# Expert blocks behind a dense layer: DMA transposes for the first three blocks, a later place for the last gate, and a list table read from another queue

## The chip, the cores and the metric

One core of a Trainium2 chip runs the kernel. The metric is the device time of one execution in microseconds; lower is better. The core's engines work in parallel and each takes its own instructions in order: TensorE (PE, matmuls; PEld are its weight loads), VectorE (DVE), ScalarE (ACT), GpSimd (POOL) and SyncE (SP, which here only issues transfers). Sixteen DMA engines carry out the transfers that SyncE and GpSimd issue.

## The reference: what is computed

```python
x = attention(q, k, v)                 # 4 x 8 heads, 576 positions, decaying mask, no softmax -> [2304, 512]
x = softplus(x @ w_in) @ w_out         # dense layer, 512 -> 2048 -> 512
logits = x @ w_gate                    # 8 experts
noisy = logits + log1p(exp(x @ w_noise)) * noise
top2 = argpartition(-noisy, 2, axis=1)[:, :2]
w = exp(top2_logits - max);  w /= w.sum() + 1e-9
for e in range(8):                     # each token goes to two experts
    h = maximum(x[mask_e] @ w1[e], 0)  # 512 -> 1024
    out[mask_e] += w[mask_e] * (h @ w2[e])
```

## The kernel before

The 2304 tokens are worked in six tiles of 384 (`NTILE`, `TT`). Numbers that need float32 are held as a high and a low half in float16, and a product is three matmuls (high with high, low with high, high with low).

**The dense layer.** `g1` and `g2` run tile by tile in a list of steps. When a tile's rows are done, `x2_done` (three times, j = 0 to 2) writes them as float16 rows, has SyncE transpose them by DMA into `x2t` and store them in the DRAM tensor X2. `logits(t)` multiplies the transposed rows with the gate's weights (36 matmuls of 16 columns, L432), takes the top two, builds `M` (which experts a token takes) and the running counts `mc`, and the exp and reciprocal for the weights. `ranks(t)` turns counts into each token's place in its expert's list (six matmuls, L471 and L472), and GpSimd scatters six columns of entries (token, weight) into the DRAM `table` (L504).

**The lists.** `schedule(first, n)` turns the counts into a list of blocks: for each block its table column, its expert's place and whether its weights have to be loaded. It is made twice: list a holds the first `NBA` = 5 blocks and is made from the counts of five of the six tiles, list b holds the other 39 and is made when the last tile's counts are known. In both cases the whole table is read into `tab` (L603, 380 KB, on SyncE).

**The expert blocks.** A block is 128 entries of one expert, some 36 to 44 in all. `prep(i)` copies the block's entries out of `tab` on GpSimd (L646), gathers the rows from X2 (L649), and has SyncE transpose them by DMA into `xt` (L655, 128 x 1024 float16). `e1(i)` is the first layer: two halves of 12 matmuls (L668), each evicted by ScalarE as the high part (L673) and by VectorE as the low part (L674) of `hr`, interleaved; then VectorE transposes `hr` into `ht` with 16 instructions (L680). `e2(i)` is the second layer, 24 matmuls (L689) on `ht`, and `combine(i)` scales the result on ScalarE (L700) and adds it to the output with an indirect DMA on GpSimd (L701). `weights(i, half)` is a 2 MB load on SyncE under a condition (L637): it moves bytes only where the block's expert differs from that of the block before. `e2` lags `e1` by three blocks (`LAG`).

**What sets the order.** The instructions are traced in program order; a planner then fills each engine's queue by its own model of times: of the instructions that it takes to be ready it takes the one traced first. So later work may be put ahead of earlier work that is not ready by that model. `tc.issue_after(x)` puts the instructions of a block behind `x` on the same engine, and `behind("sync")` puts them behind the last instruction noted as `LAST["sync"]`, here a DMA transpose. Around the change the program traces: the last rows of the dense layer, `prep(0)` to `prep(3)` (`PA` = 4) with the first weight load between, `logits(5)`, block 0's `e1`, weight loads, `ranks(5)`, block 1's `e1`, one more `prep`, list b with block 2's `e1` in its middle, and then the loop over blocks.

Of the kernel before, what the change touches and what calls it, by code (L numbers as in the profile page):

```python
# [10 lines left out]
F32 = mybir.dt.float32  # L11
F16 = mybir.dt.float16
# [4 lines left out]
AF = mybir.ActivationFunctionType  # L17
ALU = mybir.AluOpType

B, H, S, D = 4, 8, 576, 64  # L20
NT, DM, FF = 2304, 512, 2048
NE, F2 = 8, 1024
# [9 lines left out]
NBLK = 2 * NT // P + NE  # L32
NB = NT // P
NBA = 5
NTAIL = 3
NCOL = NE * NB + NBLK + 2

# [43 lines left out]
def body(ctx, tc, ins, out):  # L81
# [324 lines left out]
    MC = {0: rt.tile([P, 4, NE], F16, name="mc", bufs=2)}  # L406
    nc.vector.memset(MC[0], 0.0)

    XT2, RT, STORE, SCAT = {}, {}, {}, {}

    def x2_done(t, j):
        end = t == NTILE - 1
        rows = E["ep"].tile([P, 2, DM], F16, name="rows", bufs=3) if end else ring("rows", 1, 0, [2, DM], F16, 3)
        p2 = PG.pop((t, j))
        k = S_X2 / (S_G * S_WO)
        nc.scalar.activation(rows[:, 0], p2, AF.Copy, scale=k)
        nc.vector.scalar_tensor_tensor(out=rows[:, 1], in0=p2, scalar=k, in1=rows[:, 0], op0=ALU.mult, op1=ALU.subtract)
        r = rows.rearrange("p a d -> p (a d)")
        xt = E["ep"].tile([P, 8, P], F16, name="x2t", bufs=3) if end else ring("x2t", 1, 6144, [8, P], F16, 3)
        nc.sync.dma_start_transpose(out=xt, in_=r)  # L420
        t0 = t * TT + j * P
        STORE[t, j] = nc.sync.dma_start(out=X2[t0:t0 + P, :], in_=r)
        XT2[t, j] = xt

    def logits(t):
        lg = ps.tile([P, 3, 16], F32, tag="sm", name="lg", bufs=1)
        for j in range(3):
            xt = XT2.pop((t, j))
            n = 0
            for k in range(KC):  # L430
                for a, b in ((0, 0), (0, 1), (1, 0)):
                    nc.tensor.matmul(lg[:, j, :], lhsT=xt[:, a * 4 + k, :], rhs=wg[:, b, k, :], start=n == 0, stop=n == 11)  # L432
                    n += 1
        s = 1.0 / (S_X2 * S_WG)
        ns = rt.tile([P, 3, NE], F32, name="ns", bufs=2)
        nc.scalar.activation(ns, lg[:, :, 8:16], AF.Exp, scale=s)
        nc.scalar.activation(ns, ns, AF.Ln, bias=1.0)
        nc.vector.tensor_tensor(out=ns, in0=ns, in1=noise[:, 3 * t:3 * t + 3, :], op=ALU.mult)
        nl = rt.tile([P, 3, NE], F32, name="nl", bufs=2)
        nc.vector.scalar_tensor_tensor(out=nl, in0=lg[:, :, 0:8], scalar=s, in1=ns, op0=ALU.mult, op1=ALU.add)  # L440
        mx = rt.tile([P, 3, NE], F32, name="mx", bufs=2)
        ix = rt.tile([P, 3, NE], U32, name="ix", bufs=2)
        for j in range(3):
            nc.vector.max(out=mx[:, j], in_=nl[:, j])
            nc.vector.max_index(out=ix[:, j], in_max=mx[:, j], in_values=nl[:, j])
        ef = rt.tile([P, 3, 2], F32, name="ef", bufs=2)
        nc.vector.tensor_copy(ef, ix[:, :, 0:2])
        oh = rt.tile([P, 3, 2, NE], F16, name="oh", bufs=2)
        nc.vector.tensor_tensor(out=oh, in0=iota[:, None, None, :NE].to_broadcast([P, 3, 2, NE]),
                                in1=ef[:, :, :, None].to_broadcast([P, 3, 2, NE]), op=ALU.is_equal)  # L450
        M = rt.tile([P, 3, NE], F16, name="M", bufs=2)
        nc.vector.tensor_tensor(out=M, in0=oh[:, :, 0], in1=oh[:, :, 1], op=ALU.add)
        mc = MC[t]
        for j in range(3):
            nc.vector.tensor_tensor(out=mc[:, j + 1], in0=mc[:, j], in1=M[:, j], op=ALU.add)
        MC[t + 1] = rt.tile([P, 4, NE], F16, name="mc", bufs=2)
        nc.vector.tensor_copy(MC[t + 1][:, 0], mc[:, 3])

        ed = rt.tile([P, 3, 4], F32, name="ed", bufs=2)
        nc.vector.tensor_tensor(out=ed[:, :, 0], in0=mx[:, :, 1], in1=mx[:, :, 0], op=ALU.subtract)  # L460
        nc.scalar.activation(ed[:, :, 1], ed[:, :, 0], AF.Exp)
        nc.vector.tensor_scalar(ed[:, :, 2], ed[:, :, 1], 1.0, 1e-9, op0=ALU.add, op1=ALU.add)
        nc.vector.reciprocal(ed[:, :, 3], ed[:, :, 2])
        RT[t] = (ef, oh, M, ed)

    def ranks(t):
        ef, oh, M, ed = RT.pop(t)
        mc = MC.pop(t)
        pr = ps.tile([P, 3, NE], F32, tag="sm", name="pr", bufs=1)
        for j in range(3):  # L470
            nc.tensor.matmul(pr[:, j], lhsT=before, rhs=M[:, j], start=True, stop=False)  # L471
            nc.tensor.matmul(pr[:, j], lhsT=ones, rhs=mc[:, j], start=False, stop=True)  # L472
        qe = rt.tile([P, 3, NE], F32, name="qe", bufs=2)
        nc.vector.tensor_tensor(out=qe, in0=pr, in1=e4k[:, None, :].to_broadcast([P, 3, NE]), op=ALU.add)
        pq = rt.tile([P, 3, 2, NE], F32, name="pq", bufs=2)
# [43 lines left out]
    def schedule(first, n, between=lambda: None):  # L519
# [80 lines left out]
            LIST["more"] = ni[0:1, 0:1]  # L600
            nc.vector.tensor_scalar(ni[:, 0:1], red(nb[:, None, :]), float(n - NTAIL), None, op0=ALU.is_gt)
        tab = E["ep"].tile([P, NCOL * 4], I32, name="tab", bufs=1)
        nc.sync.dma_start(out=tab, in_=table.rearrange("(p c) f -> p (c f)", p=P))  # L603
        return bi, tab


# [48 lines left out]
        LAST["sync"] = nc.sync.dma_start_transpose(out=xt, in_=xr)  # L655
        TI[i], XE[i] = ti, xt

    def e1(i):
        ep, r, xt = E["ep2"], REG[i], XE.pop(i)
        hr = ep.tile([P, 2 * F2], F16, name="hr", bufs=3)  # L660
        pair = hr.rearrange("p (f a) -> p f a", a=2)
        M1[i] = []
        for n in range(2):
            ph = E["eps" if i < NBA else "eps2"].tile([P, 512], F32, name="ph", bufs=2)
            m = 0
            for k in range(KC):
                for a, b in ((0, 0), (1, 0), (0, 1)):
                    M1[i].append(nc.tensor.matmul(  # L668
                        ph, lhsT=xt[:, a * 4 + k, :], rhs=AR[0][:, ds(r * 8192 + (b * 4096 + k * 1024 + n * 512), 512)],
                        start=m == 0, stop=m == 11))  # L670
                    m += 1
            hi, lo = (pair[:, n * 512:(n + 1) * 512, a] for a in range(2))
            LAST["act"] = nc.scalar.activation(hi, ph, AF.Relu)  # L673
            nc.vector.scalar_tensor_tensor(out=lo, in0=ph, scalar=0.0, in1=hi, op0=ALU.max, op1=ALU.subtract)  # L674
        ht = ep.tile([P, 2 * F2], F16, name="ht", bufs=5)
        src = hr.bitcast(F32).rearrange("p (c q f) -> p c q f", c=8, q=4)
        dst = ht.bitcast(F32).rearrange("p (c q t) -> p c q t", c=8, q=4)
        for f in range(4):
            for t in range(4):
                nc.vector.transpose(dst[32 * f:32 * f + 32, :, t], src[32 * t:32 * t + 32, :, f])  # L680
        HT[i] = ht.rearrange("p (c t a) -> p c t a", c=8, a=2)

    def e2(i):
        r, ht = REG[i], HT.pop(i)
        py = E["eps" if i < NBA else "eps2"].tile([P, DM], F32, name="py")
        M2[i] = []
        for c in range(8):
            for a, b in ((0, 0), (1, 0), (0, 1)):
                M2[i].append(nc.tensor.matmul(  # L689
                    py, lhsT=ht[:, c, :, a], rhs=AR[1][:, ds(r * 8192 + (b * 4096 + c * 512), 512)],  # L690
                    start=len(M2[i]) == 0, stop=len(M2[i]) == 23))
        PY[i] = py
# [77 lines left out]
        a L b g g a L b g g a L b g A6 g a L b g g a L b g g S6 a b g g Q6 a b g K6 g a V6 b r  # L770
        g g g g
    """.split()
    PA, PB = 4, 2
    QE = 5 * NS + 7
    def step():
        u = order.pop(0)
# [39 lines left out]
    preps = list(range(PA, NMAIN))  # L816

    def first(i):
        e1(i)
        place(i + 1)  # L820


    logits(NTILE - 1)
    with tc.issue_after(LAST["g2"].ins):
        place(0)
    first(0)
    weights(0, 1)
    weights(3, 0)
    weights(3, 1)
    weights(4, 0)  # L830
    ranks(NTILE - 1)
    first(1)
    prep(preps.pop(0))
    LIST["b"] = schedule(False, NBLK - NBA, lambda: first(2))
    ps_s.close()
# [3 lines left out]
    for i in range(2, NMAIN + LAG):  # L839
        j = i - LAG  # L840

        def second():
            e2(j)
            combine(j)
            if j + 4 < NMAIN:
                weights(j + 4, 1)

        early = i == NMAIN - 1
        if early:
            second()  # L850
        if 2 < i < NMAIN:
            e1(i)
            if i + 1 < NMAIN:
                place(i + 1)
            if i + 4 < NMAIN:
                weights(i + 4, 0)
        if j >= 0 and not early:
            second()
        while preps and preps[0] <= i + AHEAD + 1 and (preps[0] < NBA or i >= PB):
            prep(preps.pop(0))  # L860
            if preps and preps[0] == NBA + 2 and i == PB:
                break
    weight_deps()
    with tc.If(nc.values_load(LIST["more"], min_val=0, max_val=1) > 0):  # L864
        for i in range(NMAIN, NBLK):
            LAST.clear()
            weights(i, 0)
            weights(i, 1)
            prep(i)
            REG[i] = nc.tensor.value_load(entry(i, 1), min_val=0, max_val=2)  # L870
            e1(i)
            e2(i)
            combine(i)

# [24 lines left out]
```

## Time and profile before

| | |
|---|---|
| Median of three runs | 935.3 us (934.69 to 936.69) |
| The profiled execution | 935.35 us |
| Its span, first to last instruction | 933.4 us |
| TensorE busy | 890.1 us, 95% of the span |
| VectorE busy | 674.5 us, 72% |
| ScalarE, GpSimd busy | 383.3 us, 257.3 us |
| Mean granted TensorE clock | 0.983 of full speed |
| VectorE transposes of hr (L680) | 656 instructions, 285.9 us |

All times within the execution are microseconds from the start of the span. "Idle before" is the time in which an engine had nothing to do ahead of an instruction, and the arrow names what ended that time. The granted clock is the share of full speed at which TensorE was let run in a stretch. A busy share is an average over a stretch, so the stretches are looked at one by one.

### The profile page before, as it was taken

How to read it: one execution, taken by the hardware profiler on the slowest of the kernel's cores; microseconds unless marked ns; L12 is line 12 of the kernel's file. 1: busy time of each engine (PE TensorE's matmuls, PEld its weight loads, DVE VectorE, ACT ScalarE, POOL GpSimd, SP SyncE). 2: the span in 40 equal slices, each digit the busy share in tenths (PEclk: the TensorE clock that was granted, in tenths of full speed). 3: DMA queues.
4: the chain of work that ended last, by engine and by line, in shares of the span. 5: the costliest groups of instructions: out<-in, count | busy, mean ns of one | idle time of the engine just before them, and what ended most of it. 6: DMA issues, size and time to landing. Idle time of an engine off the chain costs nothing. (4 is left out here: it accounts for less than half of the span.)

```text
span 933.4 us, 17302 instructions
## 1 busy us (share of the span) xinstructions
PE 890.1 (95%) x5370; PEld 460.1 (49%) x5370; DVE 674.5 (72%) x1415; ACT 383.3 (41%) x595; POOL 257.3 (28%) x237
## 2 busy tenths in 40 slices
PE   7989999999999999999967799999999999999996
PEld 6654555555555555555523344444444444444442
DVE  5597958776886874444529989888788878887881
ACT  3689857666775773454411112212221222122121
POOL 3666533300411400201302242223222322232112
PEclk9999999999999999999979999999999999999999
DMA  9859999999999982002380366778456765776412
GB/s 355 337 192 279 308 318 399 344 273 392 369 323 366 388 292 50 1 17 52 142 225 13 84 114 92 187 230 166 72 137 188 173 161 159 203 207 163 119 24 33
DMA packets 134983, 185.52 MB, mean 199 GB/s; under 512 B 73776, under 2 KB 82992, under 8 KB 132848
## 3 DMA queue, kind: packets, MB, share of 16 engines
q1 hardware_dynamic: 124560, 164.11, 55.0%
q0 software_dynamic: 10336, 20.27, 11.1%
q8 instruction: 52, 0.85, 0.4%
q14 instruction: 35, 0.29, 0.1%
HBM read 246.01 MB, written 54.20 MB: 322 GB/s over the span
## 5 line engine op out<-in xcount | busy, mean ns | idle before, releaser
L680 DVE STREAM_TRANSPOSE ht<-hr 32x256 f32<-32x256 f32 x656 | 285.9, 436 | 12.5
L668 PE MATMUL ph<-w,xt 128*128 x984 | 224.4, 385 | 4.1 <-DVE hr L674 3.3
L689 PE MATMUL py<-w,ht 128*128 x984 | 219.1, 379 | 4.9 <-DVE ht L680 3.2
L301 PE MATMUL pg<-x,wi 128*128 128x384 f16 x1152 | 203.4, 326 | 4.3 <-ACT a L311 1.9
L332 PE MATMUL p<-w,g 128*128 128x512 f16 x864 | 201.3, 380 | 2.2 <-POOL w L161 2.2
L668 PEld LDWEIGHTS <-xt 128*128 128x128 f16 x984 | 97.0, 99 | 123.0 <-issue 10.8
L689 PEld LDWEIGHTS <-ht 128*128 128x128 f16 x984 | 96.2, 98 | 121.5 <-DVE ht L680 3.6
L301 PEld LDWEIGHTS <-wi 128*128 128x128 f16 x1152 | 111.4, 98 | 88.3 <-issue 3.8
L701 POOL DMA_INDIRECT out_dram<-y,ti x41 | 64.9, 1584 | 292.3 <-ACT y L700 271.8
L673 ACT ACTIVATE hr<-ph 128x512 f16<-128x512 f32 x82 | 60.8, 742 | 183.0 <-PE ph L668 159.2
L332 PEld LDWEIGHTS <-g 128*128 128x128 f16 x864 | 82.3, 98 | 95.1 <-issue 5.5
L674 DVE SCALAR_TENSOR_TENSOR hr<-ph,hr 128x512 f16<-128x512 f32 x82 | 59.3, 729 | 70.1 <-ACT hr L673 56.4
L357 DVE SCALAR_TENSOR_TENSOR w<-w 128x1024 f16<-128x1024 f32 x64 | 81.1, 1269 | 37.9 <-ACT w L356 34.7
L700 ACT ACTIVATE y<-py,ti 128x512 f32<-128x512 f32 x41 | 28.2, 687 | 177.0 <-PE py L689 172.5
L315 DVE SCALAR_TENSOR_TENSOR r<-a,r 128x768 f32<-128x768 f32 x48 | 53.7, 1119 | 55.7 <-ACT a L314 55.0
L356 ACT ACTIVATE w<-w 128x1024 f16<-128x1024 f32 x64 | 67.4, 1054 | 62.1 <-DMA w<-in_moe_w_dram 40.2
L504 POOL DMA_INDIRECT table<-tb,pos x36 | 43.8, 1217 | 169.1 <-DVE pos L489 160.0
L310 ACT ACTIVATE r<-pg 128x384 f32<-128x384 f32 x96 | 46.4, 484 | 72.5 <-PE pg L301 69.5
L649 POOL DMA_INDIRECT xr<-X,ti x41 | 43.3, 1057 | 19.6 <-POOL ti L646 11.3
L311 ACT ACTIVATE a<-pg 128x384 f32<-128x384 f32 x96 | 46.6, 486 | 0.0
L313 ACT ACTIVATE a<-a 128x768 f32<-128x768 f32 x48 | 40.4, 842 | 1.2
L314 ACT ACTIVATE a<-a 128x768 f32<-128x768 f32 x48 | 40.3, 840 | 0.9
(129 smaller groups left out, 594.0 us busy)
## 6 DMA issues: line engine op xcount, KB each, us to landing
w<-wsc SPq DMA_DIRECT2D x78, 2048.0 KB
w<-in_moe_w_dram SPq DMA_DIRECT2D x64, 512.0 KB
wsc<-w SPq DMA_DIRECT2D x64, 512.0 KB
qk<-in_qk_dram SPq DMA_DIRECT2D x18, 512.0 KB
kv<-in_kv_dram SPq DMA_DIRECT2D x18, 512.0 KB
w<-in_moe_w_in_dram SPq DMA_DIRECT2D x8, 1024.0 KB
w<-in_moe_w_out_dram SPq DMA_DIRECT2D x8, 1024.0 KB
out_dram<-zero SPq DMA_DIRECT2D x1, 4608.0 KB
```

Of the source, the lines that this page charges most:

```text
L301: nc.tensor.matmul(pg, lhsT=wi[:, a, k, f * P:(f + 1) * P], rhs=x[:, b, k, :], start=n == 0, stop=n == 11)
L311: nc.scalar.activation(a[:, i], pg, AF.Abs)
L315: nc.vector.scalar_tensor_tensor(out=r, in0=a, scalar=S_G, in1=r, op0=ALU.mult, op1=ALU.add)
L332: m = nc.tensor.matmul(PG[t, j], lhsT=g[:, a, f % 2, j * P:(j + 1) * P], rhs=wo[b][:, f, :], start=f == 0 and a + b == 0, stop=f == NFB - ...
L356: nc.scalar.activation(h[:, 0], t, AF.Copy, scale=s)
L357: nc.vector.scalar_tensor_tensor(out=h[:, 1], in0=t, scalar=s, in1=h[:, 0], op0=ALU.mult, op1=ALU.subtract)
L668: M1[i].append(nc.tensor.matmul(ph, lhsT=xt[:, a * 4 + k, :], rhs=AR[0][:, ds(r * 8192 + (b * 4096 + k * 1024 + n * 512), 512)], start=m = ...
L673: LAST["act"] = nc.scalar.activation(hi, ph, AF.Relu)
L674: nc.vector.scalar_tensor_tensor(out=lo, in0=ph, scalar=0.0, in1=hi, op0=ALU.max, op1=ALU.subtract)
L680: nc.vector.transpose(dst[32 * f:32 * f + 32, :, t], src[32 * t:32 * t + 32, :, f])
L689: M2[i].append(nc.tensor.matmul(py, lhsT=ht[:, c, :, a], rhs=AR[1][:, ds(r * 8192 + (b * 4096 + c * 512), 512)], start=len(M2[i]) == 0, st ...
L701: LAST["pool"] = nc.gpsimd.indirect_dma_start(out=out[:, :], out_offset=bass.IndirectOffsetOnAxis(ap=ti[:, 1:2], axis=0), in_=y[:, :], in_ ...
```

## The change

For blocks 0 to 2 (`NFIRST` = 3), `hr` is written with its high half first and its low half behind, and SyncE transposes it by one DMA of 128 x 2048 into `ht`; later blocks keep VectorE's transposes. `e1` is split into its two halves, `e1(i, 0)` and `e1(i, 1)`. The last tile's `logits` is traced behind block 0's `e1` and the first half of block 1's, and is put behind that half's last matmul on TensorE; `ranks` of that tile is put behind block 1's last matmul. The last tile's three stores to X2 are traced behind its three transposes. The exp and reciprocal of the weights move from `logits` to `ranks`. `PA` goes from 4 to 3, so blocks 3 and 4 are prepared behind `ranks`. `py` gets two buffers while the first five blocks run. The list table is read from GpSimd's queue instead of SyncE's. Since `LAST["sync"]` is now also set by the DMA transposes of `hr`, the weight loads traced behind block 0's `e1` come behind that transpose on SyncE.

```diff
+NFIRST = 3
...
     def x2_done(t, j):
...
         nc.sync.dma_start_transpose(out=xt, in_=r)
         t0 = t * TT + j * P
-        STORE[t, j] = nc.sync.dma_start(out=X2[t0:t0 + P, :], in_=r)
+        KEPT.append((t, j, t0, r))
         XT2[t, j] = xt
+        if not end or j == 2:
+            for t, j, t0, r in KEPT:
+                STORE[t, j] = nc.sync.dma_start(out=X2[t0:t0 + P, :], in_=r)
+            KEPT.clear()
...
     def logits(t):
...
-        ed = rt.tile([P, 3, 4], F32, name="ed", bufs=2)
-...
-        RT[t] = (ef, oh, M, ed)
+        RT[t] = (ef, oh, M, mx)
...
-        nc.sync.dma_start(out=tab, in_=table.rearrange("(p c) f -> p (c f)", p=P))
+        nc.gpsimd.dma_start(out=tab, in_=table.rearrange("(p c) f -> p (c f)", p=P))
...
-    def e1(i):
+    def e1(i, n):
+        ep, r, xt = E["ep2"], REG[i], XE[i]
+        if n == 0:
+            HR[i] = ep.tile([P, 2 * F2], F16, name="hr", bufs=3)
+            M1[i] = []
+        hr = HR[i]
+        parts = hr.rearrange("p (f a) -> p a f", a=2) if i >= NFIRST else hr.rearrange("p (a f) -> p a f", a=2)
...
+        hi, lo = (parts[:, a, n * 512:(n + 1) * 512] for a in range(2))
         LAST["act"] = nc.scalar.activation(hi, ph, AF.Relu)
         nc.vector.scalar_tensor_tensor(out=lo, in0=ph, scalar=0.0, in1=hi, op0=ALU.max, op1=ALU.subtract)
+        if n == 0:
+            return
+        XE.pop(i)
         ht = ep.tile([P, 2 * F2], F16, name="ht", bufs=5)
+        if i < NFIRST:
+            LAST["sync"] = nc.sync.dma_start_transpose(out=ht.rearrange("p (c t) -> p c t", c=16), in_=hr)
+            HT[i] = ht.rearrange("p (a c t) -> p c t a", a=2, c=8)
+            return
...
-        py = E["eps" if i < NBA else "eps2"].tile([P, DM], F32, name="py")
+        py = E["eps" if i < NBA else "eps2"].tile([P, DM], F32, name="py", bufs=2)
...
-    PA, PB = 4, 2
+    PA, PB = 3, 2
...
-    logits(NTILE - 1)
     with tc.issue_after(LAST["g2"].ins):
         place(0)
     first(0)
+    e1(1, 0)
+    with tc.issue_after(M1[1][11].ins):
+        logits(NTILE - 1)
     weights(0, 1)
     weights(3, 0)
     weights(3, 1)
     weights(4, 0)
-    ranks(NTILE - 1)
-    first(1)
+    e1(1, 1)
+    place(2)
+    with tc.issue_after(M1[1][-1].ins):
+        ranks(NTILE - 1)
+    prep(preps.pop(0))
     prep(preps.pop(0))
     LIST["b"] = schedule(False, NBLK - NBA, lambda: first(2))
```

## Rows read from the trace of the kernel before

**Rows 1.** Windows: length, busy PE, PEld, DVE, ACT, POOL, granted clock, DMA share, GB/s.

```profile
473.40:541.60 68.20, 49.00 (x238) 21.01 (x237) 51.27 (x166) 9.74 (x16) 15.44 (x19) 0.87 0.41 101
541.60:925.10 383.50, 383.48 (x1777) 173.67 (x1775) 304.82 (x652) 79.40 (x110) 98.91 (x99) 1.00 0.61 146
```

**Rows 2.** Timeline of TensorE from 462 to 560: start, duration, instructions.

```profile
473.53 2.75 PE L668 MATMUL ph<-w,xt 128*128 x12
...
489.40 0.45 PE L432 MATMUL lg<-wg,x2t 128*128 128x16 f16 x12
...
501.25 0.17 PE L546 MATMUL pc<-mc,ones 128*128 128x8 f16 x1
...
541.59 10.52 PE L668 MATMUL ph<-w,xt 128*128 x48
```

**Rows 3.** Timeline of the tile before: its gate, counts, ranks and positions.

```profile
427.70 1.05 PE L432 MATMUL lg<-wg,w 128*128 128x16 f16 x36
...
431.79 0.17 DVE L457 COPY mc<-mc 128x8 f16<-128x8 f16 x1
...
436.39 0.17 PE L471 MATMUL pr<-M,before 128*128 128x8 f16 x1
...
439.36 0.17 DVE L489 SCALAR_TENSOR_TENSOR pos<-qi 128x6 int32<-128x6 int32 x1
```

**Rows 4.** Waits of TensorE from 473.4 to 541.6: us in total, times, longest.

```profile
PE lg L432 <- DMA x2t<-rows: 8.2, 1, 8.2
PE ph L668 <- DVE hr L674: 3.3, 1, 3.3
PE py L689 <- DVE ht L680: 3.2, 1, 3.2
PE pr L471 <- DVE M L452: 1.8, 1, 1.8
PE py L689 <- ACT y L700: 1.7, 2, 0.8
```

**Rows 5.** Windows behind the three long waits: busy time, granted clock, DMA share.

```profile
484.50:489.00 4.50, 4.50 (x35) 2.06 (x36) 0.00 (x0) 0.00 (x0) 0.00 (x0) 0.55 0.82 230
501.00:506.00 5.00, 4.96 (x17) 1.94 (x18) 4.87 (x21) 0.00 (x0) 1.19 (x2) 0.66 0.00 0
526.70:530.00 3.30, 3.29 (x9) 1.21 (x9) 3.23 (x9) 0.00 (x0) 2.43 (x4) 0.57 0.26 79
```

**Rows 6.** Timeline of SyncE's queue, 474 to 515: issues.

```profile
475.28 0.36 SPq L637 DMA_DIRECT2D w<-wsc  x1
475.70 1.24 SPq L420 DMA_TRANSPOSE x2t<-rows  x1
...
480.20 3.28 SPq L420 DMA_TRANSPOSE x2t<-rows  x1
...
491.75 1.27 SPq L655 DMA_TRANSPOSE xt<-xr  x1
```

**Rows 7.** Groups of VectorE's instructions from 501.2 to 525.9.

```profile
L680 DVE STREAM_TRANSPOSE ht<-hr 32x256 f32<-32x256 f32 x32 | 13.9, 436 | 0.5
L674 DVE SCALAR_TENSOR_TENSOR hr<-ph,hr 128x512 f16<-128x512 f32 x4 | 2.8, 721 | 0.0
```

**Rows 8.** Windows around the row transpose issued at 491.75.

```profile
488.70:493.00 4.30, 4.30 (x33) 2.06 (x30) 2.53 (x16) 1.05 (x4) 0.00 (x0) 1.00 0.01 3
493.00:495.00 2.00, 0.32 (x2) 0.00 (x0) 1.86 (x8) 0.78 (x2) 0.00 (x0) 1.00 0.70 130
```

**Rows 9.** Timelines of GpSimd and SyncE, 500 to 536: table and block 5.

```profile
504.51 1.02 POOL L504 DMA_INDIRECT table<-tb,pos  x1 [31.81 <-DVE pos L489]
...
513.18 0.35 SPq L603 DMA_DIRECT2D tab<-table  x1
...
525.92 0.18 POOL L646 COPY ti<-tab 128x4 int32 x1 [3.90 <-DVE bib L598]
...
531.64 2.62 SPq L655 DMA_TRANSPOSE xt<-xr  x2
```

More of the change, by code (lines that the diff above doesn't have):

```diff
@@ L407, in body @@
     nc.vector.memset(MC[0], 0.0)
-    XT2, RT, STORE, SCAT = {}, {}, {}, {}
+    XT2, RT, STORE, SCAT, KEPT = {}, {}, {}, {}, []
     def x2_done(t, j):
@@ L457, in logits, with ranks @@
         nc.vector.tensor_copy(MC[t + 1][:, 0], mc[:, 3])
+        RT[t] = (ef, oh, M, mx)
+    def ranks(t):
+        ef, oh, M, mx = RT.pop(t)
+        mc = MC.pop(t)
+        pr = ps.tile([P, 3, NE], F32, tag="sm", name="pr", bufs=1)
+        for j in range(3):
+            nc.tensor.matmul(pr[:, j], lhsT=before, rhs=M[:, j], start=True, stop=False)
+            nc.tensor.matmul(pr[:, j], lhsT=ones, rhs=mc[:, j], start=False, stop=True)
         ed = rt.tile([P, 3, 4], F32, name="ed", bufs=2)
@@ L463, in logits @@
         nc.vector.reciprocal(ed[:, :, 3], ed[:, :, 2])
-        RT[t] = (ef, oh, M, ed)
[L466 to L472, printed above, removed]
         qe = rt.tile([P, 3, NE], F32, name="qe", bufs=2)
@@ L656, in prep @@
         TI[i], XE[i] = ti, xt
-    def e1(i):
[L659 to L674, printed above, removed]
+    HR = {}
+    def e1(i, n):
[5 more added lines that the diff above has]
+        parts = hr.rearrange("p (f a) -> p a f", a=2) if i >= NFIRST else hr.rearrange("p (a f) -> p a f", a=2)
+        ph = E["eps" if i < NBA else "eps2"].tile([P, 512], F32, name="ph", bufs=2)
+        m = 0
+        for k in range(KC):
+            for a, b in ((0, 0), (1, 0), (0, 1)):
+                M1[i].append(nc.tensor.matmul(
+                    ph, lhsT=xt[:, a * 4 + k, :], rhs=AR[0][:, ds(r * 8192 + (b * 4096 + k * 1024 + n * 512), 512)],
+                    start=m == 0, stop=m == 11))
+                m += 1
+        hi, lo = (parts[:, a, n * 512:(n + 1) * 512] for a in range(2))
+        LAST["act"] = nc.scalar.activation(hi, ph, AF.Relu)
+        nc.vector.scalar_tensor_tensor(out=lo, in0=ph, scalar=0.0, in1=hi, op0=ALU.max, op1=ALU.subtract)
+        if n == 0:
+            return
+        XE.pop(i)
         ht = ep.tile([P, 2 * F2], F16, name="ht", bufs=5)
+        if i < NFIRST:
+            LAST["sync"] = nc.sync.dma_start_transpose(out=ht.rearrange("p (c t) -> p c t", c=16), in_=hr)
+            HT[i] = ht.rearrange("p (a c t) -> p c t a", a=2, c=8)
+            return
         src = hr.bitcast(F32).rearrange("p (c q f) -> p c q f", c=8, q=4)
@@ L818, in first @@
     def first(i):
-        e1(i)
+        e1(i, 0)
+        e1(i, 1)
         place(i + 1)
-    logits(NTILE - 1)
     with tc.issue_after(LAST["g2"].ins):
@@ L851, in body @@
         if 2 < i < NMAIN:
-            e1(i)
+            e1(i, 0)
+            e1(i, 1)
             if i + 1 < NMAIN:
@@ L870, in body @@
             REG[i] = nc.tensor.value_load(entry(i, 1), min_val=0, max_val=2)
-            e1(i)
+            e1(i, 0)
+            e1(i, 1)
             e2(i)
```

## The prediction, made before the changed kernel was run

> **What bounds the kernel now.** I read the page's busy tenths by slice first: TensorE is full nearly everywhere, with a hole in the middle, where the dense layer hands over to the expert blocks. Then windows on both sides of the hole's end [rows 1]: the reader is to see that from 541.6 to 925.1 us TensorE is busy 383.48 of 383.50 us at clock 1.00, and from 473.4 to 541.6 only 49.0 of 68.2 at 0.87. Behind 541.6 nothing can be gained or hidden; if the full part starts earlier, the end moves one for one. The full part starts with the matmuls at 541.59, block 5, the first of the second list; the hole begins with block 0 at 473.53 [rows 2].
>
> What must TensorE do in the hole? L668 and L689 issue 192 matmuls there: five first layers and three second layers of 24. One costs 383.5/1777 = 0.216 us in the full part [rows 1], so 41.4. The gate's 36 small ones took 1.05 for the tile before [rows 3]; seven more small ones I put at 0.4. That is 42.9 of 68.2: **25.3 us can be gained at most**, which would give 910.
>
> Where do they go? TensorE's waits [rows 4]: 8.2 us for the gate's transposed rows, 3.3 for VectorE's hr, 3.2 for VectorE's transposes, 1.8 for M, twice 0.8 for the eviction of py: 18.2. The rest is clock: behind the three long waits the granted clock is 0.55, 0.66 and 0.57 in stretches of 4.5, 5.0 and 3.3 us [rows 5]. Length times what is missing from 1 is 2.0 + 1.7 + 1.4 = 5.1 us. Together 23.3 of the 25.3.
>
> **The parts of the change.**
>
> *The gate's transposes and block 0's W2.* SyncE issued block 0's 2 MB of second-layer weights at 475.28 and the first gate transpose at 475.70; the next one came only at 480.20 [rows 6], and TensorE stood 8.2 us. In the change that load is traced behind block 0's hr transpose, which needs hr: e1(0) ends at 473.5 + 24 x 0.216 = 478.7, and an eviction and a lo part of 0.72 each [rows 7] bring hr to about 480.4. So the three gate transposes go out with no weights ahead of them, the stores behind. The gate's matmuls now stand behind one and a half blocks, at 473.5 + 36 x 0.216 = 481.3. A transpose of 128x1024 issued at 491.75 [rows 6] moved its bytes between 493 and 495, with nothing before [rows 8]: 2.6 us to landing, 3.3 at most. Three in a row land by 481 if the first is out by 476. The wait and its clock go: **10.2 us**. A late transpose would bring the wait back at full length, since TensorE takes nothing out of order.
>
> *Three blocks of DMA transposes.* VectorE loses 48 transposes of 436 ns [rows 7], 20.9 of its 51.3 busy us in the stretch [rows 1]. What stays, 30.4, fits into a hole of some 48. The waits for ht (3.2) and hr (3.3, as the lo part queues behind transposes) go with the clock behind them (1.7 + 1.4): **9.6 us**. In their place stand DMA transposes of 128x2048, which no row shows. The nearest is the 128x1024 one: twice 2.6, about 5 us to landing, is my price. The bounds are 2.6 (the halves overlap) and 8.8 (what the first gate transpose took behind 2 MB, 475.70 to 484.48). ht(0) lands at about 485.5, at worst 489; e2(0) comes, in program order, behind e1(2) and e1(3), at about 495. Hidden. W2 leaves SyncE at about 483.5; its bytes took at worst until 488 when three transposes and stores ran along, 12.7 us from 475.3 (the DMA share was still 0.82 from 484.5 to 489.0 [rows 5]), so 496 at worst: 0 to 2 us of waiting. If it were placed ahead of e1(3), as bits of it were before, the wait would be that much. No other weights stand ahead of ht(1) and ht(2): three more weight issues stood before the transpose at 491.75, and the DMA share from 488.7 to 493.0 was 0.01 [rows 8], so their condition was false. SyncE stands at ht(i) until hr(i) exists, and behind it are the row transposes of blocks 3 and 4; at worst they follow ht(2), at 495 to 498, and TensorE has e2(0) to do meanwhile.
>
> The Trainium skill (VectorE: DVE Perf Modes, The three transpose paths) speaks against this part: 1309 ns for a 128x128 square by DMA, 311 by VectorE. By an estimate from that page a block's 16 squares take 20.9 us. The row's 8 squares took 2.6, so the trace does not agree; its time is the third rival.
>
> *Two buffers for py.* The two waits for ScalarE's eviction go: **1.7 us**.
>
> *The wait for M.* Ranks' matmuls stand behind e1(1). For the tile before, the last count was ready at 431.96, 4.3 us after the gate's matmuls began [rows 3]; here that is 485.6, and e1(1) ends at 481.3 + 1.05 + 2.6 = 485. So 0.6, or the old 1.8 with an eviction in between: I keep 1.8, nothing gained. Moving the weights' exp behind them costs nothing; the scatters alone want it.
>
> *The list table by GpSimd.* SyncE no longer stands before it. The first list's table has cover, VectorE's making of that list. For the second: ranks' matmuls to pos took 3.1 us (436.39 to 439.53) [rows 3], so pos is at 489.5; from first scatter to table 8.7 [rows 9], landing taken as the transpose's 2.6: 501. GpSimd's issue of a plain transfer no row shows; between SyncE's 0.35 and its own scatter's 1.02 [rows 9] I take 1: 502. Behind it on GpSimd stand the gathers that need it and scatter-adds, whose y has three buffers.
>
> *What is late next: block 5.* It needs list, gather and row transpose. From the count at 501.25 [rows 2] to the gather's copy at 525.92 [rows 9] VectorE gave 13.9 us to transposes and 2.8 to lo parts [rows 7]; the list, with ranks' rest, took the other 8.0. Now the count comes at about 488: 8.0, two blocks' lo parts (2.9) and 0 to 16 transposes of block 3 (7.0) give 499 to 506. From copy to row transpose took 5.7 [rows 9], landing 2.6: xt(5) at 510.5 (the table's 502 binds) to 514.5. TensorE reaches e1(5) at 473.5 + 42.9 less e2(2) (5.2) plus the 2.6 kept (M, and a wait of 0.8 in the list) at 513.8, or at 519 if e2(2) is placed first, as it was. A new wait of 0 to 2; with W2's 0 to 2 I take 1.5 for both.
>
> **The sum.** 10.2 + 9.6 + 1.7 - 1.5 = 20.0. The profiled execution took 935.35 us, its span 933.4 and 1.95 around it, 0.05 off the median of 935.3. 935.35 - 20.0 = **915.4**. With 0 to 4 us for the two new waits and 1.2 less for M the forecast's own range is 912.5 to 919.
>
> **Rivals.**
>
> *The list becomes the bound.* VectorE's queue takes all transposes of blocks 3 and 4 (14.0 us) and a third block's lo parts (1.4) into the list: ready at 514.3, xt(5) at 522.6. With e1(5) placed ahead of e2(2) TensorE waits from 513.8, 8.8 us, and 1.5 more of clock: 8.8 + 1.5 in place of 1.5, **924**; with e2(2) first 3.6 + 1.5, 919. For it: in the trace, list operations and transposes alternate. Against: two blocks' transposes compete with the list, not five.
>
> *Only the gate's lead goes.* If the path from the gate's end to block 5 stays as long as it was (489.85 to 541.59 [rows 2]), the gain is that lead, 489.85 - 482.4 = 7.5: **927.9**. For it: no order of blocks passes the list. Against: 20.9 us of VectorE's work leave just that path.
>
> *Slower: the DMA transpose costs like separate squares.* Place: SyncE's queue, ht(0) to ht(2) in turn from 480.4. At T per block e2(2) ends at 480.4 + 3T + 5.2; before, it ended at 541.6. From T = 18.7 it is slower; eight times the row's 2.6 makes T 20.8 and e2(2) 6.4 later: **942**. Against: half a block in 2.6.
>
> *It does nothing:* e2(0) waits for a W2 that lands past 515. That is over 30 us behind its issue, for a load that had landed in 12.7 with everything beside it; hardly possible.
>
> **How the numbers follow.** Chances: forecast (to 919) 0.58; list as bound (919 to 925) 0.22; gate alone (925 to 933) 0.11; no change 0.03; slower 0.06. A measurement of this kernel tells 0.2%, 1.9 us, from no change: faster 0.91, same 0.03, slower 0.06. The range goes from 911, nearly all of the hole, to 926, past the first rival; it leaves out less than 0.2.
>
> **What the profile would show.** Right: no wait for x2t, L432 near 481, clock 1.00 from 473 to 515, ht landing within 5 us of its issue, block 5 at 519 to 524 and 383 us of unbroken matmuls behind it. Wrong: a wait over 5 us before block 5 for xt or the list (first rival), block 5 at about 534 (second), ht more than 15 us behind its issue (third), or holes in the full part, which this argument takes as untouched.

## The result, and the profile after

The changed kernel takes 913.4 us in the median of four runs (911.85 to 914.59), the kernel before 936.0 beside it: a ratio of 0.976, with a 95% interval of 0.973 to 0.978. The medians lie 22.6 us apart. The prediction was 915.4, with a range of 911 to 926. The profiled execution took 914.59 us, 20.8 less than the profiled one of before; its span is 912.4 and its mean granted clock 0.992.

How late the dense layer ends differs by a few us from profile to profile: in those of this study block 0's first matmul starts between 470.7 and 474.0, though no edit touches the dense layer's matmuls. So profiles are compared from that matmul to the end of the span: 933.4 - 473.53 = 459.87 before [rows 2], 912.4 - 473.10 = 439.30 after. That is **20.6 us**, all of the gain.

The windows of the kernel after, cut at block 0's first matmul and at block 5's (columns as in rows 1):

```profile
473.10:521.30 48.20, 44.47 (x242) 20.59 (x241) 31.66 (x120) 8.99 (x16) 16.53 (x20) 1.00 0.88 178
521.30:904.00 382.70, 382.12 (x1771) 172.96 (x1769) 304.09 (x650) 79.51 (x110) 98.83 (x99) 1.00 0.60 146
```

Beside [rows 1] the hole is 20 us shorter, the clock in it 1.00 in place of 0.87, VectorE's work 31.66 in place of 51.27, and the DMA share 0.88 in place of 0.41. From block 5 on the kernel after is 0.7 us shorter (391.07 against 391.81), as six matmuls more of the second layers stand ahead of block 5; nothing else of the gain is in the full part. All of TensorE's waits from 473.1 to 560 (total, times, longest), beside [rows 4]:

```profile
PE py L704 <- DMA w<-wsc: 1.9, 1, 1.9
PE lg L437 <- DMA x2t<-rows: 1.8, 1, 1.8
PE ph L676 <- DVE hr L682: 0.6, 1, 0.6
```

Of 18.2 us there and 0.8 in the list 4.3 are left. Where they stand shows TensorE's timeline (start, duration, instructions, idle time before and what ended it):

```profile
473.10 7.93 PE L676 MATMUL ph<-w,xt 128*128 x36
480.87 0.75 PE L437 MATMUL lg<-wg,x2t 128*128 128x16 f16 x24
483.38 0.46 PE L437 MATMUL lg<-wg,x2t 128*128 128x16 f16 x12 [1.76 <-DMA x2t<-rows]
...
494.14 5.34 PE L704 MATMUL py<-w,ht 128*128 x24 [1.95 <-DMA w<-wsc]
499.32 10.52 PE L676 MATMUL ph<-w,xt 128*128 x48
509.68 11.82 PE L704 MATMUL py<-w,ht 128*128 x54
521.33 10.52 PE L676 MATMUL ph<-w,xt 128*128 x48
531.69 4.05 PE L704 MATMUL py<-w,ht 128*128 x18
```

The gate begins behind one and a half blocks, at 480.87, and waits only for its third transpose. Block 5 starts at 521.33, with the second layers of blocks 1 and 2 and a bit of block 3's (54 matmuls) ahead of it. SyncE's queue:

```profile
474.61 1.29 SPq L421 DMA_TRANSPOSE x2t<-rows  x1
475.95 0.57 SPq L427 DMA_DIRECT2D X<-rows  x1
476.62 1.29 SPq L421 DMA_TRANSPOSE x2t<-rows  x1
477.97 0.56 SPq L427 DMA_DIRECT2D X<-rows  x1
478.62 2.80 SPq L421 DMA_TRANSPOSE x2t<-rows  x1
...
483.54 1.72 SPq L688 DMA_TRANSPOSE ht<-hr  x1
485.64 6.29 SPq L642 DMA_DIRECT2D w<-wsc  x4
...
509.28 3.06 SPq L660 DMA_TRANSPOSE xt<-xr  x2
```

Three things are to be seen. The stores (L427) stand between the transposes, though the program traces them behind: the planner pulled them ahead, as it did with block 3's preparation, so neither that edit nor `PA` = 3 shows in this stretch (e2 below has neither, and the same alternation of transposes and stores). W2 (the first of the x4; the other three have a false condition) follows block 0's hr transpose. And the row transposes of blocks 5 and 6 go out from 509.28 on, 12 us ahead of block 5. What both DMA waits share is this window, from the first gate transpose to the landing of W2:

```profile
474.60:494.10 19.50, 15.81 (x109) 7.57 (x108) 11.40 (x64) 4.20 (x9) 3.56 (x4) 1.00 1.07 251
```

A share of 1.07 (it sums the time of packets, and packets can overlap) says that the DMA engines were loaded for most of the stretch. It is a mean, and there is a hole in it, while the third gate transpose was on its way and TensorE was about to wait for it:

```profile
480.00:481.00 1.00, 1.00 (x10) 0.51 (x9) 0.00 (x0) 0.00 (x0) 0.00 (x0) 1.00 2.73 116
481.00:482.00 1.00, 0.62 (x25) 0.53 (x21) 0.30 (x1) 0.60 (x1) 0.00 (x0) 1.00 0.06 15
```

In these 2 us the engines moved 116 and 15 GB/s, where the stretch has 251. e8 and e12 show the like (2.83 and 0.05; 2.66 and 0.06). What held the engines was not followed. The list's path, on GpSimd's timeline:

```profile
489.63 1.03 POOL L509 DMA_INDIRECT table<-tb,pos  x1 [17.19 <-DVE scb L534]
...
501.48 0.59 POOL L608 DMA_DIRECT2D tab<-table  x1 [3.98 <-DMA table<-tb,pos]
504.87 0.18 POOL L651 COPY ti<-tab 128x4 int32 x1 [2.79 <-DMA tab<-table]
```

### The profile page after: what moved, and what is told of

Its sections match the earlier page's. It is cut to its first block, busy times and chain, and to the rows that moved or that the text cites. A ratio compares the mean times of both kernels' runs of the same rounds, so it can differ in the third digit from the quotient of the medians.

```text
span 912.4 us, 17260 instructions
## 1 busy us (share of the span) xinstructions
PE 883.0 (97%) x5370; PEld 457.3 (50%) x5370; DVE 656.6 (72%) x1367; ACT 382.5 (42%) x595; POOL 261.0 (29%) x239
## 5 line engine op out<-in xcount | busy, mean ns | idle before, releaser
L695 DVE STREAM_TRANSPOSE ht<-hr 32x256 f32<-32x256 f32 x608 | 265.1, 436 | 11.7
L676 PE MATMUL ph<-w,xt 128*128 x984 | 218.8, 379 | 0.6 <-DVE hr L682 0.6
L316 DVE SCALAR_TENSOR_TENSOR r<-a,r 128x768 f32<-128x768 f32 x48 | 56.5, 1178 | 57.5 <-ACT a L315 56.6
```

The lines of the kernel that those rows point to most:

```text
L316: nc.vector.scalar_tensor_tensor(out=r, in0=a, scalar=S_G, in1=r, op0=ALU.mult, op1=ALU.add)
L676: M1[i].append(nc.tensor.matmul(ph, lhsT=xt[:, a * 4 + k, :], rhs=AR[0][:, ds(r * 8192 + (b * 4096 + k * 1024 + n * 512), 512)], start=m = ...
```

## The experiments

The theories. **A**, the prediction: the gate with the W2 order, and VectorE's transposes, are two causes, each worth its term. **B**: what counts is the gate's lead, got by its place behind one and a half blocks; the rest is hidden. **C**: VectorE's transposes are all of it; the gate's wait only hides VectorE's lag. **D**, **E** and **F** came up on the way and are named where they are tried. All runs, with what each came to from block 0's first matmul on:

| kernel | median us | ratio to before (95%) | block 0 to end of span | against before |
|---|---|---|---|---|
| before | | | 459.87 | |
| after | 913.4 | 0.976 (0.973 to 0.978) | 439.30 | -20.6 |
| e1 weights order | 928.4 | 0.991 (0.989 to 0.993) | 454.69 | -5.2 |
| e2 DMA transposes | 917.7 | 0.981 (0.979 to 0.983) | 442.09 | -17.8 |
| e9 transposes only | 922.5 | 0.987 (0.986 to 0.989) | 446.81 | -13.1 |
| e3 VectorE transposes | 927.3 | 0.990 (0.987 to 0.992) | 453.16 | -6.7 |
| e4 gate's place | 917.6 | 0.981 (0.979 to 0.982) | 441.67 | -18.2 |
| e11 weights early | 921.0 | 0.985 (0.983 to 0.987) | 444.70 | -15.2 |
| e5 weights ahead | 913.9 | 0.977 (0.975 to 0.979) | 439.92 | -20.0 |
| e10 and empty issues behind | 919.7 | 0.985 (0.984 to 0.986) | 443.90 | -16.0 |
| e12 empty issues behind | 919.0 | 0.983 (0.982 to 0.985) | 444.15 | -15.7 |
| e6 one DMA block | 921.4 | 0.986 (0.984 to 0.988) | 445.75 | -14.1 |
| e7 five DMA blocks | 913.0 | 0.977 (0.975 to 0.978) | 439.74 | -20.1 |
| e8 table by SyncE | 912.6 | 0.977 (0.975 to 0.978) | 439.21 | -20.7 |

The last two columns are one execution each, the medians several, and the two can differ by 2 to 3 us; differences of that size are read only where both columns show them. The kernel before ran again beside each group of runs, with medians from 934.1 to 936.0.

### Parts alone, on the kernel before

**e1: only the order of W2.** The kernel before, with the loads behind the third gate transpose on SyncE.

```diff
-        nc.sync.dma_start_transpose(out=xt, in_=r)
+        m = nc.sync.dma_start_transpose(out=xt, in_=r)
+        if end and j == 2:
+            LAST["sync"] = m
```

> The kernel before, with one edit: block 0's second-layer weights come behind the third gate transpose on SyncE. Theory A (three separate causes: the weights ahead of the gate's transposes 10.2 us, VectorE's transposes 9.6, the single py buffer 1.7): the gate now stands after 4 of block 0's matmuls, so TensorE still waits for each transpose in turn, some 5 to 6 us in all instead of 8.2, and the gate ends near 483.8 instead of 489.85; VectorE's waits stay. About 4 to 6 us faster, 930 to 932. Theory B (the gate's place behind one and a half blocks is what counts, not the queue): no change, 936. Theory C (only VectorE's load counts): no change, 936.

It gives 5.2 us, 7 in the medians, where A said 4 to 6. So the order is worth something without the rest, which neither B nor C expects. TensorE's waits from 470 to 560 say why it isn't more:

```profile
PE lg L434 <- DMA x2t<-rows: 4.1, 1, 4.1
PE py L691 <- DVE ht L682: 3.0, 1, 3.0
PE ph L670 <- DVE hr L676: 2.9, 1, 2.9
PE ph L670 <- DVE scb L551: 2.7, 1, 2.7
```

The gate's wait has halved, from 8.2, but VectorE takes a part back: the wait for an operation of the list has grown from 0.8 to 2.7.

**e2: the DMA transposes** for blocks 0 to 2, on the kernel before. Since they set `LAST["sync"]`, W2 goes behind the first of them here too.

```diff
+NFIRST = 3
...
-        pair = hr.rearrange("p (f a) -> p f a", a=2)
+        pair = hr.rearrange("p (f a) -> p f a", a=2) if i >= NFIRST else hr.rearrange("p (a f) -> p f a", a=2)
...
+        if i < NFIRST:
+            LAST["sync"] = nc.sync.dma_start_transpose(out=ht.rearrange("p (c t) -> p c t", c=16), in_=hr)
+            HT[i] = ht.rearrange("p (a c t) -> p c t a", a=2, c=8)
+            return
```

> The kernel before, with the DMA transposes of hr for blocks 0 to 2 alone; this also puts block 0's second-layer weights behind the first of them. The gate, py, the table and the order of the stores stay. Theory A: VectorE's 9.6 us go, the gate's wait shrinks from 10.2 to some 5.6, the py wait stays: 14 us faster, 920 to 924. Theory B: the gate's wait stays, 9.6 faster, 926. Theory C: the whole gain is here, 914.

17.8 us, more than A expected and less than C. This one edit, with the load order that it brings, is most of the change.

**e9: the DMA transposes without the new order.** As e2, with W2 kept where it was on SyncE, ahead of the gate's transposes. Theory E: the waits for M and the list, which A keeps, hang on VectorE's queue as well, so the transposes alone are worth more than A's 9.6.

```diff
+    weights(0, 1)
     first(0)
...
-    weights(0, 1)
     weights(3, 0)
```

> The kernel before, with the DMA transposes of hr for blocks 0 to 2 and block 0's second-layer weights kept where they were, ahead of the gate's transposes on SyncE. So VectorE's share of the change alone. Theory A (the waits simply add up): VectorE's 9.6 us go and the gate's 10.2 stay, 926. Theory E (VectorE's work is what fills the hole, and while TensorE stood for the gate VectorE stood too, so the two terms cover each other and VectorE's is the larger): 13 to 14 us faster, 921 to 922.5, as bringing the transposes back cost the changed kernel 13.9.

13.1 us, 12 in the medians: E's number. TensorE's waits from 470 to 560, all of them:

```profile
PE lg L433 <- DMA x2t<-rows: 7.9, 1, 7.9
PE py L694 <- ACT y L705: 0.8, 1, 0.8
PE pr L472 <- DVE M L453: 0.7, 1, 0.7
```

Beside [rows 4] the waits for hr and ht are gone, as A has it. But M's has also fallen from 1.8 to 0.7, one of the two for py is gone, and so is the list's 0.8: 19.0 us of waits became 9.4. The gate's stands as it was. With e1's 5.2 this makes 18.3, and e2, which has both, came to 17.8: the two parts add up.

### Parts undone, on the kernel after

**e3: VectorE's transposes for all blocks**, with W2 behind the third gate transpose, so that the order stays.

```diff
-NFIRST = 3
+NFIRST = 0
...
+        if end and j == 2:
+            LAST["sync"] = m
```

> The changed kernel with all transposes of hr on VectorE again; block 0's second-layer weights kept behind the third gate transpose. Theory A: the 9.6 us of VectorE come back, the 1.95 us wait for the weights goes or moves: 920 to 924. Theory B: nothing of the gain hangs on the transposes, 914. Theory C: all of it does, 934 to 936.

13.9 us are lost, more than A's range (920 to 924) and less than C's; e9 gained 13.1 from the other side, and B is out. Its waits from 473 to 560 and its hole:

```profile
PE ph L678 <- DVE hr L684: 6.9, 2, 3.5
PE py L706 <- DVE mx L451: 2.1, 1, 2.1
PE lg L439 <- DMA x2t<-rows: 1.5, 2, 0.9
```

```profile
480.00:535.00 55.00, 47.71 (x228) 20.65 (x227) 50.37 (x166) 7.78 (x13) 16.01 (x20) 0.88 0.52 115
```

VectorE is busy for 50.37 of 55 us. A gate that hardly waits is of little use when what follows it goes through that queue. Not all of the 13.9 is lost in the hole, though: one of the two waits for hr, 3.39 us, stands behind block 5, where after has 0.58, and the 24 matmuls behind it take 6.69 us in place of 5.34. That is some 4 us, and it returns below (the table of the gap).

**e4: the gate traced ahead of block 0**, and not tied to a matmul.

```diff
+    logits(NTILE - 1)
     with tc.issue_after(LAST["g2"].ins):
         place(0)
     first(0)
     e1(1, 0)
-    with tc.issue_after(M1[1][11].ins):
-        logits(NTILE - 1)
```

> The changed kernel with the last tile's gate traced ahead of block 0 again and not tied to block 1's matmuls; all else stays. On TensorE the gate's three parts now stand after 4, 11 and 17 matmuls of block 0. Theory A: the queue is short, so TensorE waits 2.9, 1.2 and 1.5 us for the three transposes, 5.6 in place of 1.8: 3.8 us slower, 916 to 919. Theory B: the gate's 10 us come back, 922 or more. Theory C: 914.

2.4 us are lost, 4.2 in the medians (917.6, in A's range). The planner put the gate behind 4 matmuls of block 0, and its wait for the first transpose is 3.7 in place of 1.8. The place is a small part, against B.

**e11: W2 early**, ahead of the gate's transposes on SyncE, all else as after.

```diff
+    weights(0, 1)
     first(0)
...
-    weights(0, 1)
```

> The changed kernel with block 0's second-layer weights traced ahead of block 0, so that on SyncE they stand ahead of the gate's transposes again; gate and DMA transposes stay. Theory A and E: the gate's transposes land some 5 us later than in the changed kernel, TensorE waits 6 to 7 us for them instead of 1.8, the 1.95 for the weights goes: 3 to 5 us slower, 916 to 919. Theory B (the place of the gate covers its transposes wherever they stand): 911.5 to 914.

5.4 us are lost, 7.6 in the medians (921.0, above A's range), though the gate stands behind one and a half blocks. It waits three times (2.1, 1.7 and 1.8), and the clock falls behind them; TensorE's waits and the window after the last of them:

```profile
PE lg L437 <- DMA x2t<-rows: 5.6, 3, 2.1
PE ph L676 <- DVE hr L682: 1.7, 1, 1.7
```

```profile
488.70:494.00 5.30, 5.30 (x28) 2.09 (x25) 2.45 (x23) 0.69 (x4) 0.00 (x0) 0.54 0.75 138
```

5.3 us at clock 0.54 cost 2.4; with 3.8 more of gate waits, 1.1 more for hr and no wait for W2 (1.95) that is 5.3. So the new place alone doesn't cover late transposes. But this is not the order of before either. On SyncE W2 now goes out ahead of a row transpose, that one waits for its rows until 478.77, and the gate's first transpose stands behind it, 5.5 us later than after:

```profile
471.26 0.36 SPq L642 DMA_DIRECT2D w<-wsc  x1
478.77 1.24 SPq L660 DMA_TRANSPOSE xt<-xr  x1
480.06 2.05 SPq L421 DMA_TRANSPOSE x2t<-rows  x1
```

So the 5.4 us are not the price of W2's place ahead of the gate alone.

**e8: the table read by SyncE** again (`nc.sync.dma_start` for `tab`).

> The changed kernel with the list table read from SyncE's queue again. Theory A: the table then stands behind the third DMA transpose of hr, which goes out at about 497, the scatters land at about 501, so it is read at the same time as now; block 5's rows have some 9 us to spare: no change, 912.5 to 914.5. Rival (SyncE standing before the table holds up rows and weights): 2 us or more slower.

No difference, as A says: the table's queue is worth nothing here.

### How many blocks

**e6** and **e7**: `NFIRST` = 1 and 5 in place of 3.

> The changed kernel with a DMA transpose for block 0 only; blocks 1 and 2 go back to VectorE, 32 transposes of 0.436 us. Theory A in its plain form (each transpose costs its share of 9.6 us): two thirds come back, 6.4 us slower, 920. Theory A with slack (the list and block 5's rows had some 9 us to spare in the changed kernel): a wait of 0 to 5 us for ht of block 1 and nothing for the list, 914 to 918. Rival (VectorE no longer matters once the gate is early): 913.5.

> The changed kernel with DMA transposes for blocks 0 to 4. VectorE is no longer waited for but for 0.6 us, so by theory A nothing is gained: 912.5 to 914.5. Rival (SyncE stands at hr of blocks 3 and 4 ahead of the rows of later blocks, which then come late): 2 us or more slower.

Five are no better than three: the medians are 913.0 and 913.4. One costs 6.4 us, as a plain count would have it, but not where that count would put it. No wait in the hole is long; the loss comes behind block 5, on TensorE's and VectorE's timelines of e6:

```profile
524.41 10.52 PE L676 MATMUL ph<-w,xt 128*128 x48
534.77 0.59 PE L704 MATMUL py<-w,ht 128*128 x2
539.39 8.23 PE L676 MATMUL ph<-w,xt 128*128 x24 [4.03 <-DVE hr L682]
```

```profile
531.40 7.18 DVE L695 STREAM_TRANSPOSE ht<-hr 32x256 f32<-32x256 f32 x16
538.61 1.33 DVE L682 SCALAR_TENSOR_TENSOR hr<-ph,hr 128x512 f16<-128x512 f32 x2
```

Blocks 5 and 6 run back to back (48 matmuls). VectorE takes block 5's 16 transposes, 7.18 us, ahead of block 6's lo parts, and block 7 can't start before those have freed `ph`. What TensorE has meanwhile is whatever the planner left of the second layers. Behind the wait the clock is low again, in e6's window:

```profile
541.00:546.00 5.00, 5.00 (x15) 1.81 (x14) 4.85 (x12) 0.74 (x1) 1.41 (x2) 0.57 0.82 197
```

The same place, read from the timelines of TensorE in ten kernels:

| kernel | matmuls between block 6's first layer and block 7's | wait for hr | matmuls x 0.216 + wait |
|---|---|---|---|
| e2 | 24 | none | |
| e5 | 22 | none | |
| after, e4 | 18 | 0.58, 0.57 | 4.47, 4.46 |
| e8 | 16 | 1.01 | 4.47 |
| e11 | 13 | 1.66 | 4.47 |
| e12 | 6 | 3.17 | 4.47 |
| e3 | 5 | 3.39 | 4.47 |
| e6, e10 | 2 | 4.03 | 4.46 |

The gap is 4.47 us each time, worth 21 matmuls; as many as the planner puts there are not waited for. Before, e1, e9 and e7 have 24 there and no wait; e7 has one a block later, 1.09 for hr, behind 32 of VectorE's transposes in a row. The prediction took the full part as untouchable; these are its only waits that the profiles of these kernels list from block 5 to 905 us.

### Can the last waits be had?

**e5: W2 ahead of the stores and of ht(0).** On SyncE three gate transposes, three stores, W2, and only then block 0's hr transpose. D: the DMA engines are full there, so the wait for W2 only turns into one for ht.

```diff
-        nc.sync.dma_start_transpose(out=xt, in_=r)
+        m = LAST["t2"] = nc.sync.dma_start_transpose(out=xt, in_=r)
+        if end and j == 2:
+            LAST["sync"] = m
...
-                STORE[t, j] = nc.sync.dma_start(out=X2[t0:t0 + P, :], in_=r)
+                with behind("t2"):
+                    STORE[t, j] = nc.sync.dma_start(out=X2[t0:t0 + P, :], in_=r)
...
+    weights(0, 1)
     first(0)
```

> The changed kernel with SyncE's queue in another order: the three gate transposes without stores between them, then the three stores, then block 0's second-layer weights, then the first DMA transpose of hr. Theory A (what is left of the hole is a matter of SyncE's queue): the waits of 1.8 us for the third gate transpose and of 1.95 us for the weights go, nothing comes in their place, 3 to 4 us faster than the changed kernel, 909.5 to 911, close to the bound of 910 that was worked out before. Rival D (the DMA engines are full from 473 to 494, so a wait only moves to hr's transpose or to another): no change, 912.5 to 914.5.

The time, 913.9, is D's; its reason holds for a part only. From 473 to 560 TensorE waits 1.9 for ht and 0.9 for an xt; W2's wait is gone and the gate's is 0.6. SyncE's queue in e5 shows the swap:

```profile
479.00 0.85 SPq L645 DMA_DIRECT2D w<-wsc  x1
479.94 7.33 SPq L691 DMA_TRANSPOSE ht<-hr  x1
491.21 5.12 SPq L645 DMA_DIRECT2D w<-wsc  x3
496.43 3.35 SPq L691 DMA_TRANSPOSE ht<-hr  x1
```

Behind the 2 MB the issue of ht(0) stands for 7.33 us, where it took 1.72 after; the DMA share is 0.99 from 479 to 488. TensorE doesn't wait for ht(0), though. Its 1.9 us are for ht(1), which goes out at 496.43, behind the three empty loads. These move nothing; their issues last 0.1 us or less each, but with the register instructions between them they hold the queue from 491.21 on. In that time the DMA engines stand nearly idle:

```profile
489.00:495.00 6.00, 5.84 (x28) 2.55 (x27) 5.58 (x29) 0.60 (x1) 4.52 (x5) 1.00 0.04 4
```

So this wait comes from SyncE's queue and not, as D has it, from full DMA engines.

**e10: as e5, with the three empty loads traced behind the preparation of blocks 3 and 4.** F: these loads are what is left, and with them out of the way e5 gets to 910 or 911.

```diff
-    weights(3, 0)
-    weights(3, 1)
-    weights(4, 0)
     e1(1, 1)
...
     prep(preps.pop(0))
     prep(preps.pop(0))
+    weights(3, 0)
+    weights(3, 1)
+    weights(4, 0)
```

> As the run with the weights ahead of hr's transpose, and the three weight issues of blocks 3 and 4, whose condition is false here, traced behind the preparation of blocks 3 and 4. In that run SyncE gave them 5.1 us ahead of the second DMA transpose of hr, and TensorE waited 1.85 us for that and 0.9 for the rows behind it. Theory F (what is left of the hole is the order of SyncE's queue): these waits go and nothing replaces them, 910 to 911.5. Rival D (the DMA engines themselves are full): 912.5 to 914.5 again.

Neither time came: it is 4.0 us slower than e5 from block 0 on, 6 in the medians. The two waits that F names are gone, but others came. TensorE waits 3.1 for ht(0), which stands behind W2 as in e5 (the DMA share is 1.11 from 480 to 488), and 4.0 for hr at block 7, with 2 matmuls in the gap of the table above.

**e12: the same move on the kernel after**, without e5's order.

> The changed kernel with only the three empty weight issues of blocks 3 and 4 traced later. In the changed kernel hr's second transpose, which stands behind them, has more than 10 us to spare, so nothing changes by theory F: 912.5 to 914.5. If SyncE's time as such is short, 911.5 or less.

Missed as well: 4.9 us slower than after. The waits for SyncE's transfers are hardly changed. TensorE's timeline:

```profile
525.02 10.52 PE L676 MATMUL ph<-w,xt 128*128 x48
535.38 1.46 PE L704 MATMUL py<-w,ht 128*128 x6
540.01 7.03 PE L676 MATMUL ph<-w,xt 128*128 x24 [3.17 <-DVE hr L682]
```

With the loads traced later the planner places the second layers otherwise, and 6 matmuls are left for the gap in place of 18. That is 2.6 us of wait, 1.5 of clock (0.70 from 541 to 546) and 0.4 more for W2, 4.5 of the 4.9. How the planner comes to it was not followed. So F and D each hold for a part: the wait behind the empty loads is the queue's (e5), the one for ht(0) behind W2 goes with full DMA engines (e10). That either would bring the kernel to 910 is not shown: no version measured here is faster than the changed kernel by more than the runs vary.

## Why the prediction came out right, point by point

**The bound and the sum hold.** 20.0 us were forecast, 20.6 came in the profiles (22.6 in the medians). The forecast's own range is a little wide of its terms: with 4 us for the new waits they give 917.9, not 919. TensorE's hole was read rightly as all there is to gain: the three waits that are left, 1.76 + 1.95 + 0.58, taken off the profiled 914.59, give 910.3, and the bound worked out from before was 910.

**VectorE's transposes: 9.6 forecast, 13.1 measured alone (e9), 13.9 undone (e3).** Of e3's, some 4 lie behind block 5, where the prediction saw nothing to lose; e9's are all in the hole, where block 5 comes 54.95 us after block 0 in place of 68.06. So the term was too small. The mechanism was right, its reach was not: the prediction kept 1.8 for M and 0.8 for the list as not gained, and put both waits for py down to the buffers. e9 has neither new buffers nor a new gate, and there 1.1, 0.8 and 0.9 of them went. M and the list are made by VectorE too.

**The gate and the W2 order: 10.2 forecast, 7.6 measured.** The order alone gives 5.2 (e1), the place 2.4 (e4). Three transposes were to land by 481 if the first was out by 476. It was out at 474.61, but the stores stood between them (in e5, without that, 0.6 of the wait is left), the third one's issue took 2.80 us, and TensorE had its data at 483.38. That wait of 1.76 was in the prediction put at nothing. With the 13.1 the parts make 20.7, against 20.6 for the whole: too much for the one, too little for the other, and the two errors cancelled. That the total came out so close is luck to that extent.

**py's buffers: 1.7 forecast, at most 0.8.** Behind the DMA transposes one wait of 0.8 is left (e2, e9), and with the buffers none. The buffers alone were not run.

**The DMA transpose of 128x2048: about 5 us, bounds 2.6 to 8.8.** ht(0) was issued at 483.54, W2 behind it at 485.64, and at 494.14 both were there; its own landing no row of after shows. Two waits show one: e5's ht(1) was there 5.5 us after its issue began (501.96), with idle DMA engines ahead of it, and e10's ht(0), behind 2 MB, after 11.6 (491.62), above the bound. What a transpose takes of the engines can be estimated from windows. From block 0 to block 5 share times length was 0.41 x 68.2 = 28.0 us before [rows 1]; e9, with three transposes of 128x2048 more, had

```profile
473.70:528.74 55.04, 45.56 (x237) 20.36 (x235) 32.84 (x121) 9.04 (x16) 15.45 (x19) 0.91 0.66 154
```

36.3, so 2.8 us of all sixteen engines per block (the bytes fit: 154 x 55.04 is 1.6 MB more than 101 x 68.2, three times 0.5); after, with 0.88 x 48.2 = 42.4 in a more crowded stretch, it is 4.8. The slower rival, which needs 18.7 us per block, is out. The Trainium skill (VectorE: DVE Perf Modes, The three transpose paths) gives 1309 ns for one 128x128 square by DMA, an estimate of 20.9 us for a block's sixteen; the runs don't bear that out for sixteen squares in one transfer (5.5 us, e5).

**The new waits: 1.5 forecast for W2 and block 5 together.** W2's came, 1.95 of the 0 to 2. Block 5's didn't: VectorE's last list operation ends at 497.4, ahead of the 499 to 506, so the transposes of blocks 3 and 4 stood behind the list and not in it. It was the rival with the list as bound that put them in it. The table came at 504.9 and not at 502: from the first scatter to the read's issue it took 11.9 us, with 4.0 of waiting for the last scatter, where the prediction took over the 8.7 of before. The issue and the landing, 0.59 and 2.8, were near the 1 and 2.6 assumed; block 5's transpose at 509.28 had some 9 us to spare. Of the signs, block 5 at 521.33 (519 to 524), the gate at 480.87 (near 481) and the clock of 1.00 came. "No wait for x2t" did not, with 1.76, nor did the unbroken full part.

**The other rivals.** The gate's lead alone (927.9) would have left the path from gate to block 5 at 51.7 us; it is 521.33 - 483.84 = 37.5. That it does nothing needed a W2 past 515; it came at 494.

**The step that was wrong without harm:** the full part as untouched. It has a wait of 0.58 after, and in five experiments 1.7 to 4.0. The prediction took it from the kernel before, where 24 matmuls (551.95 to 557.13) fill the gap, and didn't ask whether they would do so again.

**What stays open:** why the dense part ends up to 3 us earlier or later from one profile to the next, what held the third gate transpose, and whether an order with the last second layers kept for the gap gains the remaining 0.6 us.

## What to carry to other kernels

When an engine that works in order feeds several waits, price its relief by all of them: work taken off its queue shortens also the waits that carry other names, and another's early data is worth little as long as that queue is full. Where a hole is closed by moving work to the DMA engines, look at their share next, and where that is low (0.04 in e5) at what stands in the issuing queue. And after any edit that a planner sees, count the matmuls that cover each known gap: moving three loads that carry no bytes cost 5 us that way.

## What was not expected of the hardware

An issue on SyncE isn't of fixed length. The transpose of hr took 1.72 us to issue in the kernel after, ahead of the load of 2 MB, and 7.33 and 8.48 (e5, e10) directly behind it; whatever is queued on SyncE stands with it. A load whose condition is false still holds SyncE: three took 2.86 us in e10 and 5.12 in e5, nearly all of it between the issues. Why e5's took longer was not followed.

The clock didn't follow the length of the last wait alone. Behind e11's gate, three waits of 1.7 to 2.1 us with 12 small matmuls after each, it was 0.54, behind e6's single 4.03 it was 0.57, and behind 1.76 and 1.95 in the kernel after it stayed at 1.00; but in e8, behind a shorter wait of 1.43 at the gate, it fell, in the window from there:

```profile
481.60:486.00 4.40, 4.40 (x24) 1.72 (x20) 2.45 (x23) 0.62 (x3) 0.00 (x0) 0.61 1.09 228
```

Shares like 0.61 are means of stretches at 1.2 and at 2.4 GHz. The 1.7 us that e8 lost there cost nothing: it has no wait for W2, and its first second layer starts 20.2 us after block 0, where after has it at 21.0.
